# Three more row blocks transposed by DMA at the start of a spectral-gate and gated-MLP kernel

## The chip, the cores and the metric

The kernel runs on one core of a Trainium2 chip. The metric is the device time of one execution in microseconds (us). The kernel before takes 493.05 us, the median of three runs (492.82 to 494.5). Its profiled execution spans 490.9 us.

TensorE (PE) multiplies matrices and writes to PSUM. VectorE (DVE), ScalarE (ACT) and GpSimd (POOL) do elementwise work. SyncE (SP) issues most of the DMA transfers. A row block is 128 of the 2048 rows of the input; there are 16, numbered 0 to 15.

## The reference

x is 2048 x 576. Its rows are normalised; the result goes through a spectral filter (branch A) and through a gated MLP with a spatial mixing matrix (branch B).

```python
def _A_ref(x, w_r, w_i):
    X = rfft2(x)                      # 2048 x 289 complex
    X = X * (w_r + 1j * w_i)
    return irfft2(X).astype(bfloat16)

def _B_ref(x, w_in, w_sp, b_sp, w_out):
    z = _gelu(einsum('bsd,df->bsf', x, w_in))      # 2048 x 4608
    z1 = z[..., :Fh]                               # Fh = 2304
    z2 = _layernorm(z[..., Fh:], axis=-1)
    g = einsum('ts,bsf->btf', w_sp, z2) + b_sp[None, :, None]
    return einsum('bsf,fd->bsd', z1 * g, w_out)

xn = _layernorm(x, axis=-1)
s = _A_ref(xn, A_w_r, A_w_i)
g = _silu(_B_ref(xn, B_w_in, B_w_sp, B_b_sp, B_w_out))
return x + s * g
```

## The kernel before

The first phase normalises each row block, transposes it (the contraction over 576 columns needs the columns on partitions), and feeds it to two users on TensorE: the row transform of branch A (`p0`) and the product with the second half of w_in (`fill`, chunks of z2). The later phases do the column transforms of branch A between further chunks of branch B, then the product with w_sp (`main`), then the product with w_out (`outm`).

One large SBUF tile, AR, is cut into regions by hand. Three buffers hold normalised rows:

```python
XN = [reg("XN", i * KS * P, KS * P) for i in range(3)]
```

The loads at the start: rows 0 to 3, the first two chunks of w_in, then in three thirds the rest of w_in, each followed by a block of four row blocks of x:

```python
for g in range(3):
    third = (WIN2[:, :, 2 * g * ZC:2 * (g + 1) * ZC], slice(Fh + 2 * g * ZC, Fh + 2 * (g + 1) * ZC))
    if g:
        load_win(*third)            # two large and four small transfers on SyncE
    else:
        load_win_tail(*third, nc.gpsimd)
        load_row(3)
        nc.sync.dma_start(out=CDSD, ...)
    load_x(g + 1)                   # row blocks 4g+4 to 4g+7
```

Statistics and reciprocal root of a row block (DVE, and for row blocks from 4 on POOL), its normalisation, and the two ways to transpose it:

```python
def ln1_apply(m):
    xn = XN[m % 3]
    ...                             # two tensor_scalar on DVE: (x - mean) * rs

def xpose_dma(m):
    nc.sync.dma_start_transpose(out=xnT[:, m, :, :], in_=XN[m % 3].rearrange("p (k i) -> p k i", k=KS))

def xpose(m, eng=nc.scalar):
    xn = XN[m % 3]
    pt = psh.tile([P, KS, P], BF16, tag="h")
    for ks in range(KS):            # KS = 5
        nc.tensor.transpose(pt[:, ks, :], xn[:, ks * P:(ks + 1) * P], ident[:])
    ...                             # one eviction to xnT by ACT or DVE
```

The fold makes the sums and differences that the row transform multiplies, and `p0` multiplies them:

```python
def p0_fold(m):                     # two tensor_tensor on DVE
    xe, xo = xnT[:, m, 0:KS - 1:2, :], xnT[:, m, 1:KS - 1:2, :]
    nc.vector.tensor_tensor(out=FS[m % 4][:, 0, :, :], in0=xe, in1=xo, op=ALU.add)
    nc.vector.tensor_tensor(out=FS[m % 4][:, 1, :, :], in0=xe, in1=xo, op=ALU.subtract)

def p0(m, start):                   # four matmuls from FS[m % 4]
    ...
```

The loop over row blocks. DT is the first row block that a DMA transposes (7). The order within each of SyncE, PE and DVE is the order in which the program is written:

```python
for m in range(MT):
    if m % 2 == 0 and 0 < m < DT - 3:
        xpose(m + 3)
    spend(...)
    if m > 1:
        p0_fold(m)
    if m + 5 < MT:
        ln1_stats(m + 5, (0, 1) if m != 1 else (0,))
        if m != 1:
            ln1_aggr(m + 5)
    if m + 4 < MT:
        ln1_apply(m + 4)
        if m == 1:
            ln1_stats(m + 5, (1,))
            ln1_aggr(m + 5)
        if m + 4 >= DT:
            xpose_dma(m + 4)
        ...
    if m % 2 == 0:
        fill(1, 0)                  # four matmuls of a z2 chunk
        if m == 0:
            xpose(3)
        # p0(m), then the 64-row tails of four chunks, then the tails of p0 of m and m + 1
        fill(1, 0, lambda: p0_pair(m), lambda: p0(m, True) if m else None)
    else:
        p0(m, False)
        p0_out(m)                   # ACT evicts, POOL (or SyncE from 11 on) writes Ad
        fill(1, 0)
        if m + 3 < DT:
            xpose(m + 3)
        fill(1, 0)
```

The output stage. `outm` leaves the multiplication with y, the addition of x and the store of the last row block of an output group to a list `later`, and `main` of the next unit (one unit is seven products of eight matmuls each) works it off:

```python
prod(b, "P6", tb[u, 0])
add(p1a, b, p1)
...
prod(c, "P5", zblk(p, 0, 1))
prod(b, "P7", tb[u, 1], True)       # waits for the add above, which reads b
add(p1, b, p1b)
u_sum(1, 1, c, p1)
while later:
    later.pop()()
prod(a, "P2", zblk(p, 1, 0), True)
...
prod(c, "P3", zblk(p, 1, 1), True)
u_sum(1, 0, c, ux)
u_gate(1, 0)
tsum(u + 1, 1)
```

Of the kernel before, what the change touches and what calls it, by code (L numbers as in the profile page):

```python
# [14 lines left out]
P = 128  # L15
# [75 lines left out]
def kernel(  # L91
# [12 lines left out]
    nc = tc.nc  # L104
# [5 lines left out]
    KS = (D + P - 1) // P  # L110
# [57 lines left out]
    def reg(name, off, n):  # L168
        return AR[:, offs[name] + off: offs[name] + off + n]
# [12 lines left out]
    CESO = reg("CESO", P, 8 * QD).rearrange("p (c r d) -> p c r d", c=2, r=4)  # L182
    BF = take_(offs["G4"] + N2 * P - 8 * P, 8 * QD).bitcast(F32).rearrange("p (v a d) -> p v a d", v=2, a=2)
    MM = reg("MM", 0, 3 * P).rearrange("p (a k) -> p a k", a=3)
    XN = [reg("XN", i * KS * P, KS * P) for i in range(3)]
    YST = [reg("STG", i * D, D) for i in range(3)]
    PST = [reg("BES", i * 4 * LE, 4 * LE) for i in range(8)]
    AIN = [reg("AIN", i * 8 * L, 8 * L) for i in range(4)]
# [35 lines left out]
    def load_x(c):  # L224
        nc.sync.dma_start(out=XC[c], in_=xv[:, 4 * c:4 * c + 4, :])
# [32 lines left out]
    load_win_main(*wh[0], nc.sync, (1,))  # L258
    load_row(2)
    load_win_main(*wh[1], nc.sync, (1,))  # L260
    for g in range(3):
        third = (WIN2[:, :, 2 * g * ZC:2 * (g + 1) * ZC], slice(Fh + 2 * g * ZC, Fh + 2 * (g + 1) * ZC))
        if g:
            load_win(*third)
        else:
            load_win_tail(*third, nc.gpsimd)
            load_row(3)
            nc.sync.dma_start(out=CDSD, in_=cd_cdsd.ap().rearrange("p (a k l) -> p a k l", a=2, k=3))
        load_x(g + 1)
    def rstd_of(mv, n, tag, eng=nc.gpsimd):  # L270
        ve = small.tile([P, n], F32, tag=tag + "v")
        eng.tensor_scalar(out=ve[:], in0=mv[:, :, 1], scalar1=1e-5, scalar2=one[:, 0:1], op0=ALU.add, op1=ALU.mult)
        rs = small.tile([P, n], F32, tag=tag + "r", bufs=5)
        nc.gpsimd.tensor_tensor(out=rs[:], in0=ve[:], in1=mhalf[:, 0:n], op=ALU.pow)
        return rs
# [18 lines left out]
        ln1_stats(m)  # L294
        ln1_aggr(m)

    DT = 7
    st1 = {}
    ln1_of = {}

    def ln1_apply(m):
        xn = XN[m % 3]
        mean, rs = ln1_of[m]
        xr = XC[m // 4][:, m % 4, :].rearrange("p (a d) -> p a d", a=2)
        nc.vector.tensor_scalar(out=xn[:, 0:4 * P].rearrange("p (b a i) -> p a b i", b=2, a=2),
                                in0=xr[:, :, 0:2 * P].rearrange("p a (b i) -> p a b i", b=2), scalar1=mean, scalar2=rs,
                                op0=ALU.subtract, op1=ALU.mult)
        nc.vector.tensor_scalar(out=xn[:, 4 * P:KS * P].rearrange("p (r a i) -> p r a i", r=2, a=2),
                                in0=xr[:, None, :, 2 * P:H2].to_broadcast((P, 2, 2, HT)), scalar1=mean, scalar2=rs,
                                op0=ALU.subtract, op1=ALU.mult)  # L310

    def xpose_dma(m):
        nc.sync.dma_start_transpose(out=xnT[:, m, :, :], in_=XN[m % 3].rearrange("p (k i) -> p k i", k=KS))

    def xpose(m, eng=nc.scalar):
        xn = XN[m % 3]
        pt = psh.tile([P, KS, P], BF16, tag="h")
        for ks in range(KS):
            nc.tensor.transpose(pt[:, ks, :], xn[:, ks * P:(ks + 1) * P], ident[:])  # L319
        if eng is nc.scalar:  # L320
            nc.scalar.activation(out=xnT[:, m, :, :], in_=pt[:], func=ACT.Identity)
        else:
            eng.tensor_copy(out=xnT[:, m, :, :], in_=pt[:])  # L323
# [301 lines left out]
    def main(u):  # L625
        it, p = units[u]
        t0, nt = ITS[it]
        a, b, c = (psh.tile([P, 512], F32, tag="h", name="pm")[:, 0:nt] for i in range(3))
        B = [BB[:, h * (S // 2) + t0:h * (S // 2) + t0 + nt] for h in range(2)]
        p1, p1a, p1b, ux = (PT[4 * (u % 2) + i][:, 0:nt] for i in range(4))  # L630
        zb = Z1B[u % 2]

        def prod(dst, name, z, more=False):
            for s in range(HM):
                nc.tensor.matmul(dst, lhsT=z[:, s, :], rhs=SLB[SA[name]][:, s, 0:nt], start=(s == 0 and not more),  # L635
                                 stop=(s == HM - 1), skip_group_check=more)

        def add(out, x, y):
            nc.vector.tensor_tensor(out=out, in0=x, in1=y, op=ALU.add)  # L639

        def u_sum(f, h, x, y):
            add(U[:, 2 * p + f, h, 0:nt], x, y)

        def u_gate(f, h):
            o = U[:, 2 * p + f, h, 0:nt]
            nc.vector.tensor_tensor(out=o, in0=o, in1=zb[:, f, h, 0:nt], op=ALU.mult)  # L646

        prod(a, "P1", zblk(p, 0, 0))
        nc.scalar.activation(out=p1, in_=a, func=ACT.Identity)  # L649
        nc.gpsimd.tensor_tensor(out=p1b, in0=p1, in1=B[1], op=ALU.add)  # L650
        prod(b, "P6", tb[u, 0])
        add(p1a, b, p1)
        nc.gpsimd.tensor_tensor(out=ux, in0=p1a, in1=B[0], op=ALU.add)  # L653
        while later and not u:
            later.pop()()
        tsum(u + 1, 0)
        prod(c, "P5", zblk(p, 0, 1))
        prod(b, "P7", tb[u, 1], True)
        add(p1, b, p1b)
        u_sum(1, 1, c, p1)  # L660
        while later:
            later.pop()()
        prod(a, "P2", zblk(p, 1, 0), True)
        tsum(u + 1, 2)
        u_sum(0, 0, a, B[0])
        prod(b, "P4", tb[u, 2], True)
        u_sum(0, 1, b, p1b)
        u_gate(1, 1)
        u_gate(0, 0)
        u_gate(0, 1)  # L670
        prod(c, "P3", zblk(p, 1, 1), True)
        u_sum(1, 0, c, ux)
        u_gate(1, 0)
        tsum(u + 1, 1)

    def load_xy(m, b):
        nc.sync.dma_start(out=YIN[b], in_=Yd[m * P:(m + 1) * P, :])
# [2 lines left out]
    later = []  # L680
# [72 lines left out]
    with tc.manual_schedule(engines={SP, PE, DVE}):  # L753
# [48 lines left out]
        for m in range(MT):  # L802
            if m % 2 == 0 and 0 < m < DT - 3:
                xpose(m + 3)
            spend(0.9 if m + 3 < DT else 0.6, 0.5 + 0.6 * (m + 4 < MT) + 1.0 * (m + 5 < MT))
            if m > 1:
                p0_fold(m)
            if m + 5 < MT:
                ln1_stats(m + 5, (0, 1) if m != 1 else (0,))
                if m != 1:  # L810
                    ln1_aggr(m + 5)
            if m + 4 < MT:
                ln1_apply(m + 4)
                if m == 1:
                    ln1_stats(m + 5, (1,))
                    ln1_aggr(m + 5)
                if m + 4 >= DT:
                    xpose_dma(m + 4)
                if m + 5 == MT:
                    nc.sync.dma_start(out=G1, in_=cd_g1.ap().rearrange("p (s k) -> p s k", s=N2))  # L820
            if m % 2 == 0:
# [6 lines that stand above are left out]
                p0_out(m)  # L828
# [4 lines that stand above are left out]
# [123 lines left out]
```

## Time and profile before

| | |
|---|---|
| time, median of 3 | 493.05 us |
| span of the profiled execution | 490.9 us |
| PE busy | 483.8 us |
| DVE busy | 332.0 us |
| POOL busy | 204.6 us |
| ACT busy | 159.9 us |
| mean DMA rate | 147 GB/s |
| granted TensorE clock | 0.999 |

Reading: the profile is of one execution. A group in it is named by its line of the kernel, its engine and operation, and out<-in by the program's tile names, with the shape of one instruction and how many there are. In a list in order of time the columns are the start in us from the start of the span, the duration in us, then the group; in square brackets stands how long its engine had been idle before it and what ended that. A list of waits gives the total in us, the number of waits and the longest. PE is TensorE's matmuls, PEld its weight loads, SPq SyncE's queue of DMA issues. L329 and L330 are the fold, L305 and L308 the normalisation, L281 and L285 the statistics, L319 a transpose on PE, L321 its eviction on ACT, L347 the product of the row transform, L339 its 64-row tail, L476 the z2 chunks, L313 the DMA transposes, L354 the writes of Ad; L635 and L639 are the products and adds of `main`, L696 and L697 the deferred finish.

The two stretches that the change touches are the first 45 us and the starts of the second and third output group, near 305 and 413 us.

### The profile page before, as it was taken

Reading aid. Unit: us, or ns where it says so; the run is one execution under the profiler, and the core shown is the slowest. Engines: PE = TensorE matmul, PEld = TensorE weight load, DVE = VectorE, ACT = ScalarE, POOL = GpSimd, SP = SyncE. Lnnn points to the kernel's source line nnn. Section 1 sums busy time; section 2 is a strip of 40 time slices with the busy share of each in tenths; the row PEclk is TensorE's granted clock in tenths of the full one; section 3 lists DMA queues with packets and bytes.
Section 4 is the critical chain, followed back from the end, with each engine's and each line's share of the span. In section 5 each row is a group of like instructions: output and inputs, shape, how many; then the busy total and the mean of one; then the engine's idle time right before and its main releaser. Section 6 shows DMA issues by size and latency. Waiting matters only on the chain.

```text
span 490.9 us, 9286 instructions
## 1 busy us (share of the span) xinstructions
PE 483.8 (99%) x3407; PEld 305.9 (62%) x3407; DVE 332.0 (68%) x739; ACT 159.9 (33%) x335; POOL 204.6 (42%) x272
## 2 busy tenths in 40 slices
PE   8999999999999999999999999999999999999996
PEld 3555454555555444566665677566666678888885
DVE  7996388798876989866666527666566416877632
ACT  4767877867767565100000111000000011000001
POOL 3581134434523784454454311553553312666600
PEclk9999999999999999999999999999999999999999
DMA  8878889988464999841111996111211872111212
GB/s 279 232 142 213 254 296 278 330 237 236 133 248 121 273 257 254 278 148 33 54 44 34 184 184 161 45 34 39 59 33 43 167 174 71 52 45 46 72 38 60
DMA packets 94461, 72.13 MB, mean 147 GB/s; under 512 B 45904, under 2 KB 86608, under 8 KB 94160
## 3 DMA queue, kind: packets, MB, share of 16 engines
q1 hardware_dynamic: 88832, 57.95, 44.7%
q0 software_dynamic: 4896, 13.17, 8.2%
q8 instruction: 26, 0.43, 0.4%
q10 hardware_dynamic: 688, 0.43, 0.3%
q14 instruction: 19, 0.16, 0.1%
HBM read 40.40 MB, written 21.26 MB: 126 GB/s over the span
## 4 chain that ended last, share of the span: by engine, by line
PE 96%; DVE 2%; DMA 1%; issue 0%; SPq 0%; ACT 0%; DVEq 0%
PE pm L635 44%; PE ph L476 15%; PE ph L572 14%; PE po L691 13%; PE pa L347 2%; PE pb L404 2%; PE pa L420 1%; PE pa L446 1%; PE pa L368 1%; PE pl L691 1%; PE pa L392 1%; DMA AR<-in_A_x_dram 1%; PE pa L439 0%; DVE AR L696 0%; PE pt L319 0%; DVE AR L639 0%
## 5 line engine op out<-in xcount | busy, mean ns | idle before, releaser
L635 PE MATMUL pm<-AR,Z_74 128*128 128x384 bf16 (+1 forms) x864 | 138.8, 309 | 0.0
L639 DVE TENSOR_TENSOR AR<-pm,AR 128x384 f32<-128x384 f32 (+3 forms) x162 | 82.3, 513 | 73.7 <-PE pm L635 70.5
L635 PEld LDWEIGHTS <-Z_74 128*128 128x128 bf16 x864 | 84.5, 98 | 40.6
L635 PE MATMUL pm<-AR 128*128 128x384 bf16 (+1 forms) x648 | 107.1, 309 | 0.6 <-DVE AR L639 0.6
L476 PE MATMUL ph<-AR 128*128 128x384 bf16 (+1 forms) x480 | 87.3, 327 | 0.6 <-DVE AR L323 0.5
L572 PE MATMUL ph<-AR 128*128 128x512 bf16 (+1 forms) x360 | 84.8, 379 | 0.0
L635 PEld LDWEIGHTS <-AR 128*128 128x128 bf16 x648 | 63.3, 98 | 31.3 <-DVE AR L621 0.6
L649 ACT ACTIVATE AR<-pm 128x384 f32<-128x384 f32 (+1 forms) x27 | 12.3, 455 | 185.9 <-PE pm L635 185.9
L691 PE MATMUL po<-AR 128*128 128x288 bf16 x540 | 66.6, 286 | 0.0
L691 PEld LDWEIGHTS <-AR 128*128 128x128 bf16 x594 | 56.9, 98 | 14.0
L476 PEld LDWEIGHTS <-AR 128*128 128x128 bf16 (+1 forms) x480 | 39.6, 97 | 38.6 <-issue 16.7
L623 POOL TENSOR_TENSOR AR<-Z_74,AR 128x1024 bf16<-128x1024 bf16 x26 | 55.3, 2126 | 13.6 <-PE pm L635 12.2
L592 POOL DMA_DIRECT2D Z1d<-AR x55 | 32.0, 582 | 57.5 <-ACT AR L581 56.1
L650 POOL TENSOR_TENSOR AR<-AR 128x384 f32<-128x384 f32 (+1 forms) x27 | 22.9, 848 | 78.5 <-ACT AR L649 76.0
L581 ACT ACTIVATE AR<-ph 128x512 bf16<-128x512 f32 x72 | 41.8, 595 | 19.8 <-PE ph L572 19.6
L572 PEld LDWEIGHTS <-AR 128*128 128x128 bf16 (+1 forms) x360 | 30.3, 97 | 27.6 <-issue 4.1
L495 ACT ACTIVATE Z_74<-ph 128x384 bf16<-128x384 f32 x72 | 33.7, 498 | 20.8 <-PE ph L476 20.4
L696 DVE TENSOR_TENSOR AR<-AR 128x576 bf16<-128x576 bf16 (+2 forms) x18 | 9.7, 541 | 39.9 <-ACT AR L694 39.9
L653 POOL TENSOR_TENSOR AR<-AR 128x384 f32<-128x384 f32 (+1 forms) x27 | 30.7, 1136 | 12.9 <-DVE AR L639 12.9
L694 ACT ACTIVATE AR<-po 128x576 bf16<-128x576 f32 x15 | 9.8, 650 | 76.7 <-PE po L691 76.7
L646 DVE TENSOR_TENSOR AR<-AR 128x384 bf16<-128x384 bf16 (+1 forms) x108 | 31.3, 332 | 0.9
L699 POOL DMA_DIRECT2D out_dram<-AR x12 | 6.6, 548 | 49.9 <-DVE AR L697 42.1
(188 smaller groups left out, 472.1 us busy)
## 6 DMA issues: line engine op xcount, KB each, us to landing
Z1d<-AR POOLq DMA_DIRECT2D x55, 128.0 KB, 3.9
AR<-Z1d SPq DMA_DIRECT2D x36, 192.0 KB, 3.0
AR<-in_A_x_dram SPq DMA_DIRECT2D x20, 144.0 KB, 3.1
AR<-in_B_w_in_dram SPq DMA_DIRECT2D x14, 192.0 KB, 3.9
AR<-in_B_w_out_dram SPq DMA_DIRECT2D x1, 2592.0 KB, 11.4
AR<-Ad SPq DMA_DIRECT2D x4, 578.0 KB, 6.8
AR<-in_A_w_r_dram SPq DMA_DIRECT2D x16, 144.5 KB, 3.9
AR<-in_A_w_i_dram SPq DMA_DIRECT2D x16, 144.5 KB, 3.8
```

The lines of the kernel that those rows point to most:

```text
L476: nc.tensor.matmul(self.ph[:], lhsT=xnT[rows, self.m, ks, :], rhs=WIN2[rows, ks, n * ZC:(n + 1) * ZC], start=start, stop=stop)
L495: nc.scalar.activation(out=zc, in_=ph[:], func=ACT.Gelu_apprx_tanh)
L572: nc.tensor.matmul(self.ph[:].rearrange("p (a t) -> p a t", a=4), lhsT=wb[rows, ks, (fi % WG) * P:(fi % WG + 1) * P], rhs=xnT[rows, 4 * tq ...
L581: nc.scalar.activation(out=zs, in_=ph[:], func=ACT.Gelu_apprx_tanh)
L592: (nc.sync if place[0] > len(kinds) - 16 else nc.gpsimd).dma_start(out=d, in_=s_)
L623: (nc.gpsimd if u else nc.vector).tensor_tensor(out=t, in0=zblk(p, 1, 0), in1=t2, op=ALU.subtract)
L635: nc.tensor.matmul(dst, lhsT=z[:, s, :], rhs=SLB[SA[name]][:, s, 0:nt], start=(s == 0 and not more), stop=(s == HM - 1), skip_group_check= ...
L639: nc.vector.tensor_tensor(out=out, in0=x, in1=y, op=ALU.add)
L646: nc.vector.tensor_tensor(out=o, in0=o, in1=zb[:, f, h, 0:nt], op=ALU.mult)
L650: nc.gpsimd.tensor_tensor(out=p1b, in0=p1, in1=B[1], op=ALU.add)
L653: nc.gpsimd.tensor_tensor(out=ux, in0=p1a, in1=B[0], op=ALU.add)
L691: nc.tensor.matmul(pv[:, hh, :], lhsT=U[:, fi, h, i * P:(i + 1) * P], rhs=WOUT[:, fi, c0 + hh * H2:c0 + hh * H2 + w // nh], start=(fi == 0 ...
```

## The change

Row blocks 4, 5 and 6 are transposed by DMA instead of by PE and ACT: DT goes from 7 to 4. Normalised rows get six buffers instead of three (the three new ones lie in a region that is free until the z1 chunks). The last third of w_in, and the block of x after it, are loaded behind the transpose of row block 5 instead of ahead of all transposes. The folds of row blocks 2 and 3 move to between the statistics of a later row block and the next normalisation. In the output stage the deferred finish moves to the end of the unit. The aim is to take transposes and evictions off TensorE and ScalarE, to let the DMA transposes start before the last third of w_in fills the DMA queue, and to keep folds and the deferred finish from standing in front of what TensorE waits for.

```diff
-    XN = [reg("XN", i * KS * P, KS * P) for i in range(3)]
+    XN = [reg(n_, i * KS * P, KS * P) for n_ in ("XN", "ZT") for i in range(3)]
@@ loads
-    for g in range(3):
+    def load_third(g):
         third = (WIN2[:, :, 2 * g * ZC:2 * (g + 1) * ZC], slice(Fh + 2 * g * ZC, Fh + 2 * (g + 1) * ZC))
         ...
         load_x(g + 1)
+
+    for g in range(2):
+        load_third(g)
@@ row blocks
-    DT = 7
+    DT = 4
-        xn = XN[m % 3]
+        xn = XN[m % 6]
@@ main
         u_sum(1, 1, c, p1)
-        while later:
-            later.pop()()
         prod(a, "P2", zblk(p, 1, 0), True)
         ...
         tsum(u + 1, 1)
+        while later:
+            later.pop()()
@@ the loop over row blocks
-            if m > 1:
+            if m >= DT:
                 p0_fold(m)
             if m + 5 < MT:
                 ln1_stats(m + 5, (0, 1) if m != 1 else (0,))
                 if m != 1:
                     ln1_aggr(m + 5)
+            if 1 < m + 1 < DT:
+                p0_fold(m + 1)
             if m + 4 < MT:
                 ln1_apply(m + 4)
                 ...
                 if m + 4 >= DT:
                     xpose_dma(m + 4)
+                if m == 1:
+                    load_third(2)
```

(cut: the same change of `m % 3` to `m % 6` in both transposes)

## The prediction

> **What bounds the kernel now.** I read the page first: busy time by engine and the chain that ended last.
>
> ```profile
> span 490.9 us, 9286 instructions
> PE 483.8 (99%) x3407; PEld 305.9 (62%) x3407; DVE 332.0 (68%) x739; ACT 159.9 (33%) x335; POOL 204.6 (42%) x272
> ...
> PE 96%; DVE 2%; DMA 1%; issue 0%; SPq 0%; ACT 0%; DVEq 0%
> ```
>
> TensorE (PE) is the path: 483.8 of 490.9 us. Time can come only from work taken off PE or from its stalls, so next I asked who made PE wait, over the whole span:
>
> ```profile
> PE pw L757 <- DVE Z_74 L220: 1.2, 1, 1.2
> PE pm L635 <- DVE AR L639: 0.6, 1, 0.6
> PE ph L476 <- DVE AR L323: 0.5, 1, 0.5
> PE pa L347 <- DVE AR L329: 0.5, 1, 0.5
> PE pt L319 <- DVE AR L305: 0.3, 1, 0.3
> ```
>
> The change touches two of these waits: the 0.5 us for a fold (line 329) and the 0.6 us of the last output stage (line 639). The start (pw, first pt, first ph) stays as it is. Then PE in order of time around the fold wait:
>
> ```profile
> 18.27 0.50 PE L476 MATMUL ph<-AR 64*128 64x384 bf16 x4
> 18.61 0.41 PE L339 MATMUL pa<-AR 64*128 64x290 bf16 x4
> 19.53 0.67 PE L347 MATMUL pa<-AR 128*128 128x290 bf16 x4 [0.51 <-DVE AR L329]
> 20.04 0.81 PE L476 MATMUL ph<-AR 128*128 128x384 bf16 x4
> 20.68 0.44 PE L319 MATMUL pt<-ident,AR 128*128 128x128 bf16 x5
> 20.96 2.11 PE L476 MATMUL ph<-AR 128*128 128x384 bf16 x12
> ...
> 23.50 0.50 PE L476 MATMUL ph<-AR 64*128 64x384 bf16 x4
> ```
>
> Line 319 is the transpose of one row block. Its record lasts 0.44 us, but the next matmul starts 0.28 us after it: in the stream it costs 0.28, because tails of matmuls overlap. The tails groups (the 64-row x4 groups) beat the time, one per two row blocks: they start at 13.05, 18.27, 23.50, 27.88, 32.25. Without transposes the beat is 4.37; the two before are 5.22 and 5.23.
>
> How full the other resources are there:
>
> ```profile
> 10.00:15.00 5.00, 5.00 (x42) 2.67 (x39) 4.34 (x16) 3.01 (x7) 1.64 (x5) 1.00 1.08 322
> 15.00:20.00 5.00, 4.45 (x39) 2.65 (x39) 4.45 (x18) 3.95 (x9) 3.70 (x7) 1.00 1.10 323
> 20.00:25.00 5.00, 5.00 (x41) 3.05 (x40) 4.61 (x18) 3.50 (x8) 2.85 (x6) 1.00 0.45 115
> ```
>
> Columns: PE, weight load, DVE, ACT, POOL busy, granted clock, DMA share, GB/s. DVE is about 90% busy throughout; the DMA engines are full until 20 us, then half empty.
>
> [...]
>
> **The change on PE.** Three transposes leave (rows 4, 5, 6): 3 x 0.29 = 0.87 us. Row 4's also waited for its normalised row: the four matmuls before it start at 14.29, need 4 x 0.163 = 0.65, and the transpose starts at 15.14, so 0.2 us of stall leaves. The fold wait is worth 19.53 - 18.27 = 1.26 against the undisturbed 28.56 - 27.88 = 0.68: 0.58. Check: 0.58 + 0.2 of transposes and stall in the first long beat (excess 0.85), 0.28 + 0.58 in the second (excess 0.86). At most 0.87 + 0.2 + 0.58 = 1.65 us early. Three ACT evictions of 0.76 us also go; ACT is not on the path.
>
> **The change on DVE.** It loses no work, only order. From the start-to-start times one row block costs statistics 0.85, aggregate 0.13, normalise 0.55, fold 0.41: 1.94 us, against 4.37 / 2 = 2.19 us on PE. What held the fold of row 3 before:
>
> ```profile
> 18.64 0.41 DVE L305 TENSOR_SCALAR AR<-AR,mv_292,rs 128x512 bf16<-128x512 bf16 x1 [0.48 <-PE ph L476]
> ...
> 19.19 0.29 DVE L329 TENSOR_TENSOR AR<-AR 128x256 bf16<-128x256 bf16 x1
> ```
>
> Normalising row 6 started when POOL's rs for it ended (18.03 + 0.57 = 18.60; the named PE is a near coincidence), and the fold stood behind it. Now the fold goes first. Adding up from 15.22: half the statistics of row 6 to 15.6, fold 2 to 16.0, normalise 5 to 16.6 (data written to 16.75), rest of the statistics and aggregate to 17.1, statistics and aggregate of 7 to 18.1, fold 3 first half done 18.4. PE, 0.78 us earlier, is ready for it at 17.49 + 0.68 = 18.17. So 0.3 us of the 0.58 stays; row 3's product starts at 18.47 instead of 19.53: 1.06 us gained there. Then fold 4 at 20.6, fold 5 at 22.5, both just in time for PE (row 4 at 21.57, row 5 at 22.84); fold 6 is wanted at 24.5.
>
> **The new queue on SyncE.** Before, the transposes had an emptied queue:
>
> ```profile
> L313 SPq DMA_TRANSPOSE AR<-AR x9: 1199/1226/1792, 21.6 to 37.4; - x9
> ...
> DMA to landing us min/median/max: 2.6/4.1/6.2
> ```
>
> Now the order is transpose 4, transpose 5, two big and four small loads of the last third of w_in, the last block of x, transpose 6. Transpose 4 issues when row 4 is normalised, 15.33, and lands near 18; transpose 5 issues at 16.8 and lands near 19.5 to 20. The loads issue from 18.05, six at 0.46 us each (13.82 to 15.59 before), x at 20.8, transpose 6 at 21.25. As data: the last third took from 16.05 (landing of the x block ahead) to 19.60, 3.5 us, and x from 19.60 to 22.12, 2.5 us, beside two Ad writes. Starting near 19.4, the third is in by 22.5 to 23, x by 24.5 to 25, transpose 6 (640 packets of 256 bytes at 21 ns in the packet records: 0.85 us of 16 engines) with Ad writes beside it near 26. The third is wanted by PE only at 24.8 (row 0's fifth chunk, 26.15 before): fits.
>
> Transpose 6 does not fit. Fold 6 waits from 24.5 to 26.0, row 6's product starts at 26.35 instead of its free 26.0, and fold 7 comes one DVE row later: 26.05 + 1.94 + 0.29 = 28.3, where PE would be at 27.6. Row 7's product then starts at 28.3, against 28.56 before. After that DVE gains 0.25 us a row and PE runs free. So of 1.06 us about 0.25 is left, 0 to 1.0 for transpose 6 landing between 26.3 and 25.0.
>
> **The last output stage.** The deferred finish (lines 696, 697) moves from the middle of the next unit to its end. Before, it stood from 417.97 to 420.1, blocked by line 623 on POOL until 419.28, and the chain ran over DVE to the 0.64 us stall at 423.03. After: last gate and sum done near 421.05, finish (0.4 each) to 421.9, the add that PE waits for done at 422.35; PE wants it at 422.36. If line 650 on POOL (421.15 to 421.89) holds the finish, it ends 0.5 later. Gain 0.1 to 0.6, say 0.35. The same move at 311.6 meets units of 9.1 us with slack: nothing.
>
> **Sum.** 0.25 + 0.35 = 0.6, plus some weight on a transpose 6 that lands earlier than I add up: 0.95. 493.05 - 0.95 = 492.1.
>
> **Rivals.** First, everything goes through: no DVE wait, both stalls vanish: 1.65 + 0.6, 490.8 us. For it: DVE still leads PE by 2 us at fold 6 (25.26 against 27.29). Against: 1.5 us of queue added ahead of transpose 6. Second, the queue hits harder: Ad writes of 4 to 7 us to landing squeeze transpose 6 past 27, DVE passes the delay to every later row until it has caught up, and PE loses 1 us on balance: 494. Third, the last third of w_in comes after 24.8, and PE waits there directly: 0 to 1 us lost, while DVE catches up meanwhile: 492.5 to 493.5. Fourth, the early gain is undone later by a DMA-paced step (the reads of Ad before the first column stage): the first read lands at 56.66, its matmul starts at 57.95, so 1.3 us of slack speaks against.
>
> **Range and chances.** All of it moves within 2 us of 493, far below 2% (9.9 us). Nothing in the rest of the program changes: the order on PE differs only by the 15 matmuls. 80% range 490.8 to 493.3; faster by over 2% 0.01, same 0.98, slower 0.01.
>
> **What would show it.** Right: DVE's fold line waits 1 to 2 us for a DMA on AR near 25 us; PE's line for the row products waits for the fold at rows 6 and 7, 0.3 to 0.7 us each; the tails beat from 13 to 18.3 shrinks to 4.5; the last-stage wait for line 639 falls below 0.5. Wrong: no DMA wait on the folds (first rival), a PE wait for w_in (third), or tails groups after 32 us that are later than before (second).

## The result and the profile after

The changed kernel takes 497.11 us (median of 4 runs, 496.82 to 498.08) against 492.94 us for the kernel before on the same chip: a ratio of 1.0081, 95% interval 1.0056 to 1.0107. It is slower, by about 4 us. The predicted 492.1 us and its range, 490.8 to 493.3, both miss.

The page of the kernel after first. In part 2, PEclk is the granted TensorE clock in tenths for 40 slices of the span.

```profile
span 495.0 us, 9261 instructions
...
PE 484.7 (98%) x3392; PEld 305.8 (62%) x3392; DVE 331.2 (67%) x739; ACT 158.6 (32%) x332; POOL 204.7 (41%) x272
...
PEclk9989999999999999999999999999999999999999
...
PE 89%; DMA 6%; DVE 4%; issue 1%; POOL 0%; ACT 0%; DVEq 0%; POOLq 0%
```

TensorE has 15 matmuls fewer and yet 0.9 us more busy time; its clock is below full in the third slice (24.8 to 37.1 us), and DMA has 6% of the chain that ended last, where it had 1%. Who made PE wait (columns: us in total, times, longest):

```profile
PE pa L351 <- DVE AR L333: 3.1, 2, 2.6
...
PE pm L639 <- DVE AR L643: 0.4, 1, 0.4
```

After the load section a line of the kernel after is 4 higher than before: L351 is the row product (was L347), L333 the fold (L329), L317 the DMA transpose (L313), L343 the tails (L339), L480 the z2 chunks (L476). The fold wait, 0.5 us before, is 3.1 us now. The chain in order of time (start, us, what) says what the fold waited for:

```profile
15.50 5.72 DMA AR<-AR
...
22.36 6.57 DMA AR<-AR
...
29.37 1.15 PE pa L351 x4
```

These two DMAs are the transposes of row 4 (15.50 to 21.22) and of row 6 (22.36 to 28.93). VectorE stands still for the second one; this is the fold of row 6:

```profile
29.02 0.29 DVE L333 TENSOR_TENSOR AR<-AR 128x256 bf16<-128x256 bf16 x1 [3.86 <-DMA AR<-AR]
```

TensorE in order of time:

```profile
18.53 0.67 PE L351 MATMUL pa<-AR 128*128 128x290 bf16 x4
...
21.67 0.67 PE L351 MATMUL pa<-AR 128*128 128x290 bf16 x4
...
23.54 0.67 PE L351 MATMUL pa<-AR 128*128 128x290 bf16 x4 [0.53 <-DVE AR L333]
24.05 2.76 PE L480 MATMUL ph<-AR 128*128 128x384 bf16 x16
29.37 1.15 PE L351 MATMUL pa<-AR 128*128 128x290 bf16 x4 [2.56 <-DVE AR L333]
30.45 0.82 PE L480 MATMUL ph<-AR 64*128 64x384 bf16 x4
31.06 0.69 PE L343 MATMUL pa<-AR 64*128 64x290 bf16 x4
31.69 0.95 PE L351 MATMUL pa<-AR 128*128 128x290 bf16 x4
...
35.07 0.66 PE L351 MATMUL pa<-AR 128*128 128x290 bf16 x4
```

The L351 lines are the products of rows 3, 4, 5, 6, 7 and 8. The products of rows 6, 7 and 8 in the kernel before:

```profile
27.29 0.66 PE L347 MATMUL pa<-AR 128*128 128x290 bf16 x4
...
28.56 0.67 PE L347 MATMUL pa<-AR 128*128 128x290 bf16 x4
...
31.66 0.66 PE L347 MATMUL pa<-AR 128*128 128x290 bf16 x4
```

At row 6 the same four matmuls last 1.15 us instead of 0.66, at row 7 0.95, at row 8 0.66 again. The windows say why (columns as in the prediction; behind the five pairs of busy time stands the granted clock, 1.00 in the first line):

```profile
28.00:28.50 0.50, 0.00 (x0) 0.00 (x0) 0.00 (x0) 0.00 (x0) 0.00 (x0) 1.00 2.25 380
28.50:29.00 0.50, 0.00 (x0) 0.00 (x0) 0.00 (x0) 0.00 (x0) 0.00 (x0) 0.88 0.10 26
29.00:30.00 1.00, 0.63 (x3) 0.43 (x4) 0.97 (x4) 0.00 (x0) 0.00 (x0) 0.50 1.28 304
...
31.00:32.00 1.00, 1.00 (x8) 0.38 (x5) 1.00 (x4) 1.00 (x3) 0.81 (x1) 0.50 0.59 107
32.00:32.50 0.50, 0.50 (x5) 0.34 (x4) 0.47 (x3) 0.50 (x1) 0.03 (x1) 0.71 0.57 114
```

The starts of the row products, before and after:

| row | before | after | difference |
|---|---|---|---|
| 3 | 19.53 | 18.53 | -1.00 |
| 5 | 24.18 | 23.54 | -0.64 |
| 6 | 27.29 | 29.37 | +2.08 |
| 7 | 28.56 | 31.69 | +3.13 |
| 8 | 31.66 | 35.07 | +3.41 |
| last matmul of the program ends | 487.16 | 490.67 | +3.51 |
| span | 490.9 | 495.0 | +4.1 |

So the early gain is there. Then 2.7 us go at row 6 (2.56 of them the wait), 1.3 at the halved clock between rows 6 and 8. Behind that some 0.4 us go in the column stages (waits for the multiplies of line 398), 0.27 come back in the output stage, and the closing part after the last matmul is 0.6 us longer.

### The profile page after: what moved, and what is told of

Its sections match the earlier page's. It is cut to its first block, busy times and chain, and to the rows that moved or that the text cites. A ratio compares the mean times of both kernels' runs of the same rounds, so it can differ in the third digit from the quotient of the medians.

```text
span 495.0 us, 9261 instructions
## 1 busy us (share of the span) xinstructions
PE 484.7 (98%) x3392; PEld 305.8 (62%) x3392; DVE 331.2 (67%) x739; ACT 158.6 (32%) x332; POOL 204.7 (41%) x272
## 4 chain that ended last, share of the span: by engine, by line
PE 89%; DMA 6%; DVE 4%; issue 1%; POOL 0%; ACT 0%; DVEq 0%; POOLq 0%
PE pm L639 44%; PE po L695 13%; PE ph L576 13%; PE ph L480 12%; DMA AR<-AR 2%; DMA AR<-in_B_w_in_dram 2%; PE pa L351 1%; PE pa L424 1%; PE pb L408 1%; PE pa L450 1%; PE pa L372 1%; PE pl L695 1%; DMA AR<-in_A_w_i_dram 1%; PE pa L396 1%; DMA AR<-in_A_x_dram 1%
## 5 line engine op out<-in xcount | busy, mean ns | idle before, releaser
L480 PE MATMUL ph<-AR 128*128 128x384 bf16 (+1 forms) x480 | 87.5, 328 | 0.8 <-DVE AR L327 0.5
L480 PEld LDWEIGHTS <-AR 128*128 128x128 bf16 (+1 forms) x480 | 39.8, 97 | 39.7 <-issue 17.9
L585 ACT ACTIVATE AR<-ph 128x512 bf16<-128x512 f32 x72 | 41.9, 596 | 19.7 <-PE ph L576 19.5
L700 DVE TENSOR_TENSOR AR<-AR 128x576 bf16<-128x576 bf16 (+2 forms) x18 | 7.6, 424 | 39.9 <-ACT AR L698 39.9
L398 DVE TENSOR_TENSOR AR<-pa,AR 128x578 bf16<-128x578 f32 x32 | 22.8, 752 | 6.7 <-PE pa L396 3.9
## 6 DMA issues: line engine op xcount, KB each, us to landing
AR<-in_A_w_r_dram SPq DMA_DIRECT2D x16, 144.5 KB, 3.6
AR<-in_A_w_i_dram SPq DMA_DIRECT2D x16, 144.5 KB, 3.7
```

Source lines behind the costliest of these rows:

```text
L480: nc.tensor.matmul(self.ph[:], lhsT=xnT[rows, self.m, ks, :], rhs=WIN2[rows, ks, n * ZC:(n + 1) * ZC], start=start, stop=stop)
L585: nc.scalar.activation(out=zs, in_=ph[:], func=ACT.Gelu_apprx_tanh)
```

## The experiments

The theory in its first form: the DMA transposes land later than predicted because they share the queue and the engines with loads and with GpSimd's writes of the row products to `Ad`, and the wait that follows halves TensorE's clock. Rivals: the clock is the larger part; the last third of w_in is; the rest of the change is. Ratios are against the kernel before on the same chip (medians 493.28 to 493.49 us), with 95% intervals.

### The clock, the third of w_in, and the rest of the change

**e1_warm**: dummy matmuls ahead of row 6's product, nothing else.

```diff
-                fill(1, 0, lambda: p0_pair(m), lambda: p0(m, True) if m else None)
+                fill(1, 0, lambda: p0_pair(m), lambda: (keep_warm(10) if m == 6 else None, p0(m, True) if m else None))
```

> The changed kernel with ten 512-column matmuls on a zero tile put in front of row 6's product, where PE waits 2.56 us. They take about 2.2 us of that wait, so PE is idle at most 0.5 us at a time. Theory (the wait costs twice: 2.56 us of idle and about 1.3 us of the halved clock that follows): no slice under full clock near 30 us, the step from row 6's product to row 7's falls from 2.32 to about 1.3 us, and the time falls by 1.0 to 1.4 us to about 495.9 us. Rival (the clock record is of no account, the wait alone costs): 497.1 us or a little more.

Measured: 497.04 us, 1.0069 (1.0050 to 1.0088). The clock stays at full rate (1.00 in every window of 1 us from 12 to 40 us). Row 6's transpose lands 0.2 us later (29.13) and its product starts at 29.57; from there to row 8 (34.55) it takes 4.98 us, where the kernel after took 5.70 and the kernel before 4.37. So 0.7 of the 1.3 us belonged to the clock alone. The other 0.6 stay: with full clock, row 7's product waits for its own transpose, which lands at 30.97. Later, 0.59 us are lost in a wait for VectorE at 103.3 us. The gain of 1.0 to 1.4 us that was expected is not to be seen in the time: 497.1 us was the rival's figure. With these intervals a gain of half a microsecond could not be told.

**e2_third_first**: the last third of w_in and the x block loaded ahead of all transposes again.

```diff
-    for g in range(2):
+    for g in range(3):
         load_third(g)
@@
-                if m == 1:
-                    load_third(2)
```

> The changed kernel with the last third of w_in and the last block of x loaded ahead of all transposes, as before the change; rows 4 to 6 still by DMA. Theory (what counts is what stands ahead of a transpose in SyncE's queue): now transpose 4 is the one behind the loads: it lands near 23 to 24 instead of 21.2, fold 4 waits 3 us instead of 0.6, row 4's product waits 2 us, but transposes 5 and 6 follow it closely (25 and 26) and fold 6 waits little. Time 494 to 497 us. Rival (DMA transposes are slow in this stretch whatever stands ahead): the same waits as in the changed kernel at row 6, 497 us.

Measured: 496.88 us, 1.0077 (1.0052 to 1.0101): the loss only moves. Row 4's transpose, issued at 16.68, lands at 25.45, and TensorE waits there (the profiled execution, at 499.35 us, is the slowest of five, so these landings are late ones):

```profile
25.90 0.67 PE L351 MATMUL pa<-AR 128*128 128x290 bf16 x4 [3.06 <-DVE AR L333]
```

**e3_third_later**: the third behind the transpose of row 6 (`if m == 2` in place of `if m == 1`).

> The changed kernel with the last third of w_in one row block later, behind transpose 6. Theory of the queue: transpose 6 issues near 20 and lands by 23.5 to 24, fold 6 no longer waits; the third lands 2 us later than now, at 26 to 28, so PE waits 1 to 2 us for w_in, and transpose 7 now stands behind it, so fold 7 waits 2 to 4 us. Time 494.5 to 497.5 us, with the wait of 2.5 us at row 6 gone. Rival (transposes slow by themselves): fold 6 still waits 3 us or more and the time is over 497.5 us.

Measured: 495.43 us, 1.0043 (1.0027 to 1.0059). Row 6's transpose, with neither load ahead of it, takes 19.18 to 21.82, 2.6 us, and row 6 does not wait; but the transpose of row 4, with neither the third nor the last x block near it, still takes 15.43 to 20.83. So what delays the first transposes is not the third. TensorE now waits 0.93 us for w_in at 26.2 and 0.92 us for row 7's transpose at 29.5.

**e4_rest_alone**: the DMA transposes and the load order of before (DT = 7, third first), with the six buffers, the early folds and the moved finish.

> The rest of the change alone: rows 4 to 6 transposed by PE and the last third loaded first, as before; six buffers, the moved folds of rows 2 and 3 and the moved finish stay. Theory (all of the loss is from the three DMA transposes): no DMA wait of a fold before 35 us, the 0.5 us wait of row 3's product smaller, the wait in the last output stage 0.4 us; 0.3 to 0.9 us faster than before, 492.0 to 492.7 us. Rival (the new order costs something itself): 493.5 us or more.

Measured: 492.89 us, 0.9992 (0.9985 to 0.9998). The rest of the change is worth some 0.4 us. The whole loss comes with the three transposes.

### Ad writes beside the transposes

In the traces so far the transposes land in company: 21.22 beside an `Ad` write that lands at 21.40; in e3 20.83 and 21.36 beside one at 21.08. The packet records of the kernel after add to this: of the 640 packets of 256 bytes of row 4's transpose 548 start before 18.0, and the last has passed at 18.49, but the sixteen increments of its semaphore all come between 20.61 and 21.22. So its data had passed more than 2 us before it counted as landed, and the last increment comes 0.18 us ahead of the landing of GpSimd's write at 21.40. That the one waits for the other is the author's guess from these times. Theory A, then: the `Ad` writes hold the transposes' completion back. Rival Q: it is SyncE's own queue.

**e6_ad_late** and **e7_ad_late_third_later** were meant to issue the writes of rows 0 to 5 later:

```diff
-        (nc.gpsimd if m < 11 else nc.sync).dma_start(out=Adw[m], in_=sg[:, :, 0:L])
+        held_out.append((m, sg))
+        while m >= 6 and held_out:
+            q, s_ = held_out.pop(0)
+            (nc.gpsimd if q < 11 else nc.sync).dma_start(out=Adw[q], in_=s_[:, :, 0:L])
```

> The kernel after with one thing moved: the writes of the row products of rows 0 to 5 to Ad in DRAM are issued only once row 6's product is out, so none is in flight while the transposes of rows 4 and 5 are; nothing is left out. Theory A (the transposes' completion is held back by the Ad writes beside them): the transpose of row 4, issued near 15.5 us, lands by 18.7 instead of 21.2, row 5's by 20.0 instead of 21.6, the last third of w_in and the x block 1.5 to 2.5 us earlier, the transpose of row 6 at 26.0 to 27.0 instead of 28.9; the row product of row 6 waits under 0.7 us instead of 2.56, the clock does not halve, and the time is 493.0 to 494.6 us. Rival Q (it is the queue that the transposes stand in: the x block ahead of them, the third behind them): row 4's transpose still lands after 20.5, row 6's product still waits 2 us or more, the time is 496.3 to 497.5.

> As the run before, and the last third of w_in issued behind the transpose of row 6 as well (which alone took 495.4 us, with waits of 0.93 us for w_in at 26.2 and 0.92 us for the transpose of row 7 at 29.5). Theory A: the transposes of rows 4, 5, 6 land by 18.7, 20.0 and 22.0; the third, whose own 4.7 us are no shorter, still comes 0.5 to 0.9 us late, and row 7's transpose 0 to 0.5 late: 494.3 to 495.2 us. Rival Q: rows 4 and 5 land after 20.5 as with the third moved alone, and the time stays at 495.2 to 495.8.

They test nothing: the kernel sets only the order of SP, PE and DVE by hand, and GpSimd's first two writes still go out at 15.55 and 16.34 (e7: 15.92 and 16.71), where the kernel after has 15.64 and 16.43. 497.99 us (1.0086, 1.0070 to 1.0101) and 497.51 us (1.0078, 1.0061 to 1.0096) are readings of the kernel after and of e3 once more; that e7 is 2 us above e3 shows how far such a queue varies from build to build. Their transposes again land beside the second write: 21.32 and 21.48, 21.70 and 21.70.

**e8_ad_held** adds to the edit of e6, with the third where the kernel after has it, one copy on VectorE for which the writes truly wait:

```diff
         held_out.append((m, sg))
+        if m == 6:
+            col = AR[:, offs["BES"]:offs["BES"] + 24 * LE].rearrange("p (i c) -> p i c", c=4 * LE)[:, :, 0:1]
+            nc.vector.tensor_copy(out=col, in_=col)
         while m >= 6 and held_out:
```

> The run meant to hold the Ad writes of rows 0 to 5 back had not done so: the writes were issued at 15.6 and 16.3 us as in after, since GpSimd's instructions are placed as soon as their inputs are there. Here they truly wait: one VectorE copy of a column of the six staging buffers onto itself, placed after the sixth row's fold, must come first. Nothing is left out. Theory A (the transposes' completion is held back by Ad writes in flight): the transpose of row 4, issued near 15.5, lands by 19.0 instead of 21.2, row 5's by 20.3, the transpose of row 6 by 27.3 instead of 28.9, the row product of row 6 waits under 1 us instead of 2.56; 493.0 to 495.0 us, unless the six writes issued together near 28 us hold back the transposes of rows 9 to 11 (another 0 to 1.5 us). Rival Q (the queue in which the transposes stand, with the x block ahead and the third behind): row 4's transpose still lands after 20.5, row 6's product still waits 2 us or more, 496.5 us or more.

Measured: 499.35 us, 1.0129 (1.0112 to 1.0146), slower still, for two reasons. First, the transposes of rows 4 and 5 do land early, as A has it (15.31 to 18.55, 17.57 to 20.20), and the third's last piece at 24.56 instead of 26.20; but the x block still comes at 27.30, the transpose of row 6 at 28.03, and row 6 waits 2.49 us. For that wait Q is right. Second, the six held writes in one burst block GpSimd. Its timeline:

```profile
30.93 4.41 POOL L366 DMA_DIRECT2D Ad<-AR  x6
35.38 0.50 POOL L276 TENSOR_SCALAR ve<-mv,one 128x1 f32<-128x1 f32 x2
```

and VectorE's, where the next normalisation stands 3 us for the scale factor that GpSimd owes it:

```profile
36.44 0.41 DVE L309 TENSOR_SCALAR AR<-AR,mv,rs 128x512 bf16<-128x512 bf16 x1 [3.02 <-POOL rs L278]
```

**b5d_ad_held** and **b4d_ad_held** put the same hold into the forms with the third first (rows 5 and 6, and rows 4 to 6, by DMA).

> The form with rows 5 and 6 transposed by DMA and the third loaded first (492.34 us, waits of 0.29 and 0.10 us for row 5's transpose at 23.5) with the Ad writes of rows 0 to 5 held back in the same way. Theory A: row 5's transpose lands by 22.2 instead of 23.4, its wait is gone, 491.9 to 492.4 us. Rival Q: it lands at 23.4 as before, 492.2 to 492.7. If the held writes then collide with later transposes: a wait near 33 us and 492.8 or more.

> All three rows by DMA with the third loaded first (496.88 us, row 4's transpose 16.68 to 25.45, a wait of 3.06 us), with the Ad writes of rows 0 to 5 held back. Theory A: row 4's transpose lands by 22.3, a wait of 0 to 0.7 us instead of 3.06; 492.2 to 493.8 us. Rival Q: still behind the third and the x block, landing after 24.5, wait of 2 us or more, 495.5 to 497.5.

Measured: 493.96 us (1.0015, 1.0005 to 1.0026) and 497.24 us (1.0079, 1.0054 to 1.0103). The landings follow A: row 5's transpose in the first at 22.30 instead of 23.42, row 4's in the second at 22.18 instead of 25.45, and TensorE waits 0.64 us at row 4 instead of 3.06 (0.53 at row 5 in both). The second comparison sets the fastest of six executions beside the slowest of five, so its size is uncertain. Neither form is faster for it, and the burst shows again: waits of 1.55 us at 33.6 in the first, of 1.92 us at 35.2 in the second.

**e5_third_act_queue**: the last third from ScalarE's queue.

```diff
-                    load_third(2)
+                    load_third(2, nc.scalar)
```

> After with the last third of w_in alone issued from ScalarE's queue instead of SyncE's. Rival Q: with no third between them in its queue, the x block lands by 25.5 and the transpose of row 6 by 27.0, row 6's product waits under 0.8 us, 494.0 to 495.3 us. Theory A (and with it a common limit of the 16 engines): the transposes of rows 4 and 5 land near 21.2 and 21.6 as before whatever the queue, and the third shares the engines with the x block, so the transpose of row 6 lands at 27.5 to 29 and the time is 496.0 to 497.5 us. In either case the issue on ScalarE, 0.4 to 0.8 us each for six transfers, delays the activations near 18 to 22 us.

Measured: 498.61 us, 1.0106 (1.0083 to 1.0129), and not the test that was meant. ScalarE's place is not set by hand either: its issues moved up, the last to 13.0 us, held ScalarE, and TensorE waited for an eviction. The first of its waits (columns as above):

```profile
PE pt L324 <- ACT Z L500: 3.0, 1, 3.0
```

### Fewer transposes

**b6_one_more** and **b5_two_more**: row 6, and rows 5 and 6, by DMA, the third first, the rest of the change kept.

```diff
-    DT = 4
+    DT = 6        # and 5
+    FD = 4        # the folds of rows 2 and 3 stay early
```

> A milder form: only row 6 is transposed by DMA (before: from row 7 on), the last third of w_in and the x block loaded first as in before, folds of rows 2 and 3 moved ahead, six buffers, the moved finish of the output stage. Theory A and rival Q alike: the transpose of row 6 is issued near 19 to 20 behind an x block that lands near 20.8, comes in by 22.5 to 25.0, and its fold is not needed before 25.5, so no wait; the TensorE loses five transposes, 0.29 us, against the kernel with all the rest and no DMA transpose added (492.89 us): 492.3 to 492.9 us. If the longer closing part (0.62 us) comes with any added DMA transpose, it is 492.9 to 493.4.

> As the run before with row 5 transposed by DMA as well. Its transpose is issued near 17 behind the third of w_in and beside two Ad writes. Both theories let it come late: Q because the third (landing near 19.5) and the x block (20.8) stand ahead of it in the queue, so 22.5 to 24; A because the Ad writes land near 22 to 23 beside it. Row 5's fold is needed near 23.7: a wait of 0 to 0.8 us. Time 492.2 to 493.3 us; with a wait above 1.5 us, 493.8 or more, the transposes cost as much as in the kernel after.

Measured: 492.94 us, 0.9989 (0.9979 to 1.0000), and 492.34 us, 0.9981 (0.9970 to 0.9991). Both are slightly faster than the kernel before, but not clearly faster than e4 (0.9985 to 0.9998), which has no transpose more. The third one, row 4's, is what the kernel has no room for at the place where it stands.

### Both causes, one at a time and together

Two edits that hold back the same transfers without a burst. The x block of rows 12 to 15 goes behind the transpose of row 7:

```diff
-        load_x(g + 1)
+        if g < 2:
+            load_x(g + 1)
@@
                 if m + 4 >= DT:
                     xpose_dma(m + 4)
+                if m == 3:
+                    load_x(3)
```

and the `Ad` writes of rows 0 to 2 go out from SyncE, behind the transposes of rows 8 to 10 (`held_out` is an empty dictionary at the start):

```diff
+        if m < 3:
+            held_out[m] = sg
+        else:
+            (nc.gpsimd if m < 11 else nc.sync).dma_start(out=Adw[m], in_=sg[:, :, 0:L])
@@
+                if m - 4 in held_out:
+                    nc.sync.dma_start(out=Adw[m - 4], in_=held_out[m - 4][:, :, 0:L])
```

With the load order of the kernel after: **e9_x_behind** (x), **e11_ad_sync** (Ad), **e10_x_behind_ad_sync** (both).

> After with only the x block of rows 12 to 15 moved: issued behind the transpose of row 7 instead of ahead of the transpose of row 6. If the x block ahead of it is what holds the transpose of row 6: it lands 0.6 us after the third's last piece, near 26.8 instead of 28.9, row 6's product waits 0.3 to 0.9 us instead of 2.56, the clock keeps its full rate, 494.3 to 495.6 us. If it is the Ad write beside it (issued 21.2, landing 26.4 in after) or a common limit of the engines: the transpose lands after 28.2 all the same, a wait of 2 us or more, 496.5 us or more.

> After with only the Ad writes of rows 0 to 2 issued by SyncE behind the transposes of rows 8 to 10. If the two causes act one after the other: row 4's transpose lands by 18.7, row 5's by 20.3, the third by 25.0, the x block still ahead at 26.5 to 27.5 and row 6's transpose at 27.2 to 28.2; its product waits 1.5 to 2.5 us; 495.3 to 497.2 us. If the Ad writes alone were the cause, row 6 waits under 0.7 us: 493.3 to 494.8 us.

> As the run before, and the Ad writes of rows 0 to 2 issued by SyncE behind the transposes of rows 8 to 10 instead of by GpSimd, so no Ad write lies beside the transposes of rows 4 to 6 and GpSimd is not loaded by a burst. If the two causes are the whole of it: row 4's transpose lands by 18.7, row 5's by 20.3, the third by 24.6, row 6's transpose by 25.3, row 6's product waits under 0.2 us; 492.2 to 493.6 us, of which 0.6 is the longer closing part. If row 6 still waits over 1 us a third cause is there: 494.5 us or more.

With the third first: **b4x_x_behind** (x), **b4xa_x_behind_ad_sync** (both), and the x block moved with rows 5 and 6 only, **b5x_x_behind**.

> Rows 4 to 6 by DMA with the third loaded first (496.88 us, a wait of 3.06), only the x block of rows 12 to 15 moved behind the transpose of row 7; the Ad writes as in after. If the x block was the larger part: the transposes of rows 4 to 6 land at 21.7 to 22.3, right behind the two Ad writes (21.4, 21.6 in the form with row 4 on TensorE), a wait of 0.2 to 0.8 us at row 4, 492.4 to 493.5 us. If the Ad writes were the larger part: they land after 23 and the wait is 1.5 us or more, 494.3 us or more.

> Rows 4 to 6 by DMA, the third loaded first (496.88 us with a wait of 3.06), the x block behind the transpose of row 7 and the Ad writes of rows 0 to 2 by SyncE behind the transposes of rows 8 to 10. If both causes are the whole: row 4's transpose lands near 20.8 (0.6 after the third), rows 5 and 6 by 22, no wait of TensorE over 0.2 us, 491.6 to 492.6 us, with the longer closing part in it. If a wait over 1 us stays at rows 4 to 6 or at rows 8 to 11 (the Ad writes now in the transposes' own queue): 493.5 us or more.

> Rows 5 and 6 transposed by DMA, the third loaded first (492.34 us), with the x block of rows 12 to 15 behind the transpose of row 7. If the x block ahead is what holds row 5's transpose: it lands near 21.5 instead of 23.4, the waits of 0.29 and 0.10 us are gone, 491.8 to 492.3 us. If the Ad writes alone (landing 22.8 and 23.2) do: it lands at 23 or later, 492.2 to 492.7 us.

Measured:

| form | neither | x behind | Ad by SyncE | both |
|---|---|---|---|---|
| rows 4 to 6, third behind row 5 (after) | 1.0081 | 1.0053 (1.0038 to 1.0069) | 1.0053 (1.0036 to 1.0071) | 1.0042 (1.0027 to 1.0057) |
| rows 4 to 6, third first | 1.0077 | 1.0019 (1.0009 to 1.0029) | not run | 0.9982 (0.9973 to 0.9991) |
| rows 5 and 6, third first | 0.9981 | 0.9975 (0.9965 to 0.9985) | not run | not run |

In us, in the order of the table: 495.87, 496.54, 495.76; 494.43, 492.52; 492.33. In the first row each edit alone gains 1.4 us, and both together are not clear of either alone.

What the `Ad` writes do shows where the DMA issues of a short stretch are listed with their median us to landing. The kernel after, 15.4 to 17.4 us:

```profile
Ad<-AR POOLq DMA_DIRECT2D x2, 144.5 KB, 4.7
AR<-AR SPq DMA_TRANSPOSE x2, 5.0
```

and e10, 15.4 to 17.7 us, the same two transposes with no write beside them:

```profile
AR<-AR SPq DMA_TRANSPOSE x2, 2.9
```

So A stands for the transposes of rows 4 and 5: they land at 18.62 and 20.26 (e11: 18.99 and 20.63) instead of 21.22 and 21.57. The packet records of e10 say how much of this is the data itself: the last of row 4's 640 packets has passed at 17.98, in the kernel after at 18.49. So of the 2.6 us between the landings 0.5 lie in the data, and 2.1 between the last packet and the increments. Sharing of the engines as the data pass is thus, by these records, the smaller part. That the larger one is a wait for the write beside it is inferred from the landings (21.22 and 21.40) and from the runs without that write; how it comes about no run shows.

What the x block does shows in e9, TensorE in order of time, rows 6 and 7:

```profile
27.60 0.67 PE L352 MATMUL pa<-AR 128*128 128x290 bf16 x4 [0.57 <-DVE AR L334]
...
29.48 0.67 PE L352 MATMUL pa<-AR 128*128 128x290 bf16 x4 [0.53 <-DVE AR L334]
```

Row 6's transpose lands at 27.16, 0.7 us behind the third's last piece, instead of 28.93; the wait is 0.57 us instead of 2.56, and the clock holds (1.00 from 12 to 40 us). In e11, with the x block left ahead, that transpose lands at 29.02 although the two before it were early, and row 6 waits 2.96 us, longer than in the kernel after (waits of TensorE, columns as above; the other one is 0.53 us at row 7):

```profile
PE pa L351 <- DVE AR L333: 3.5, 2, 3.0
```

So moving the `Ad` writes does not help row 6 while the x block stands before it.

In e10 row 6 does not wait, as expected, but the time is 2 us above the expected one: the first `Ad` write left on GpSimd (row 3's, 23.34 to 27.85) now lies beside the transpose of row 7 (23.28 to 28.05), and row 7 waits 0.84 us, row 9 0.85 us, and the first column stage 0.51 us for the reads of `Ad`. The hold moved the collision by three rows. With the third first, the x block is the larger part: in b4x row 4's transpose lands at 22.03 and its product waits 0.76 us, with the `Ad` writes unmoved. And there is room for the held writes: in b4xa TensorE runs through,

```profile
21.77 0.66 PE L352 MATMUL pa<-AR 128*128 128x290 bf16 x4
...
23.36 0.67 PE L352 MATMUL pa<-AR 128*128 128x290 bf16 x4 [0.26 <-DVE AR L334]
...
26.46 0.66 PE L352 MATMUL pa<-AR 128*128 128x290 bf16 x4
...
27.73 0.67 PE L352 MATMUL pa<-AR 128*128 128x290 bf16 x4
```

rows 4 to 7 against 22.91, 24.18, 27.29 and 28.56 before. All three rows are transposed by DMA there, and the kernel is faster than before: with the two causes out of the way the three transposes are no loss at all. The form with the lowest ratio, b5x, takes 492.33 us against 493.34 of before, a quarter of a percent, and beats both kernels; its row 5 no longer waits (its transpose lands at 22.05 instead of 23.42), though its time is not clear of b5's and b4xa's.

## Why the prediction was wrong

**Right.** TensorE's early gain: row 3 at 18.53 where 18.47 was predicted, and the tails beat from 13 to 18 us is 4.37 (predicted 4.5). The kind of loss: the fold waits on a DMA near 25 us, and TensorE on the fold at row 6. The last third of w_in makes TensorE wait nowhere in the kernel after. The moved finish: the last-stage wait goes from 0.64 to 0.44 us, within the 0.1 to 0.6. That GpSimd's instructions hold the finish up is the prediction's reading, which no run tests: before, line 696 took 1.63 us beside line 623 and 0.46 us at 409.95 with GpSimd idle; after, the two instructions of the finish took 0.45 and 0.81 us, both beside line 654 on GpSimd (424.92 to 425.84).

**The step that failed** is the new queue on SyncE, the sum that ends in "transpose 6 ... with Ad writes beside it near 26". Transpose 6 landed at 28.93, and row 6's product waited 2.56 us. Two terms of the sum were too small.

The first is "Transpose 4 issues when row 4 is normalised, 15.33, and lands near 18; transpose 5 issues at 16.8 and lands near 19.5 to 20". The issues were right (15.50, 17.32, the second half a microsecond late); the landings were 21.22 and 21.57. The 2.7 us from issue to landing match the first transpose of before (21.59 to 24.27), beside which two `Ad` writes were just ending, at 22.45 and 22.88. The longer figures in the very line it quoted, up to 6.2 us, were transposes issued beside fresh `Ad` writes (29.14 to 35.32, with writes issued at 29.17 and 30.48), and it did not ask what set them apart. It named the `Ad` writes beside x and transpose 6, not beside transposes 4 and 5. Taking them away gives 18.6 and 20.3, close to the predicted landings.

The second is "the third is in by 22.5 to 23, x by 24.5 to 25". Even with both transposes on time (e8) these came at 24.6 and 27.3, and transpose 6 at 28.0. Starting from the landing of transpose 5 the third takes 4.4 us (20.20 to 24.56) where 3.5 were read off the kernel before, and x 2.7 us where 2.0 were left for it. The 3.5 us were measured from the x block ahead, with the third issued 5 us earlier, so that its first half landed 1.05 us behind that block (17.10 after 16.05); issued at 18.82, with only transpose 5 still ahead of it, the first half lands 2.3 us behind that transpose (22.47 after 20.20).

For the wait at row 6 the second term weighs more. With the first put right and x left ahead, transpose 6 still lands at 28.03 (e8) and 29.02 (e11) and row 6 waits 2.49 and 2.96 us; with x behind and the `Ad` writes left, it lands at 27.16 and row 6 waits 0.57 (e9).

**From there on** the working of the prediction carries: fold 6 stands 3.86 us (25.16 to 29.02) where 1.5 us were added up, and row 6 starts at 29.37 where 26.35 was. e9 is nearly the picture that was drawn, waits of 0.57 and 0.53 us at rows 6 and 7, but with transpose 6 landing 1.2 us later (27.16). Its last matmul ends at 488.27, 1.1 us later than before; with transpose 6 on the predicted time it would, as an estimate from these two figures, have been about level.

**Not in the prediction**: the halved clock. Rows 6 to 8 take 1.3 us longer under it, of which e1 gives 0.7 back in that stretch and nothing measurable in the time. And "Nothing in the rest of the program changes" was too strong. The wait of the column stages (0 to 1 us near 100 us) comes and goes among builds. The length of the closing part changes too: 3.71 us before, 4.33 or 4.34 in the kernel after and in seven others with its 12 DMA transposes, 3.87 to 3.98 in e5, e8 and b4d, and 3.63 in e10, e11 and b4xa, which have the same 12 transposes and the `Ad` writes of rows 0 to 2 on SyncE. So it does not come with the transposes, as some of the expectations supposed. The last store is issued 1.26 us after the last matmul both before and after, so the difference arises behind it; what sets it stays open.

**The rivals.** The second, "the queue hits harder", was the right one; its 494 us was too small because it moved transpose 6 by one microsecond and not by three, and its sign came: the tails group behind row 8's product starts at 35.66 where 32.25 was. The range treated the landing of transpose 4 as known; with 6.2 us, the longest in the quoted line, in place of 2.7 it would have reached past 496 (an estimate: 493.3 and the 3.5 us between them). The chance of staying within 2% was right, and 4 us are 0.8%.

**The budget of the experiments** (ratio less one, times 493 us): after +4.0, with the x block behind +2.6, with the `Ad` writes moved instead +2.6, with both +2.1. In the order with the third first: +3.8, +0.9, and -0.9 with both. The rest of the change alone is -0.4. So the two causes are the whole loss where the third is loaded first. In the order of the kernel after a further 2 us stay; e10 shows waits of that size at rows 7 and 9 and at the reads of `Ad`, but no run takes them away. Where the `Ad` writes are moved, 0.7 us of the gain is the shorter closing part. The conclusion for the third first does not hang on it: the last matmul ends at 486.90 in b4xa, at 487.07 in e4 and at 487.16 before.

## What to carry to other kernels

A transpose by DMA took 2.6 us here with nothing else under way (b4d, row 8) and 5.4 to 5.9 us beside two writes of 144.5 KB (e3, e6, after): before moving one to an earlier place, list what else is in flight between its issue and the time its result is needed, writes of other engines' queues too, and take its duration from a transpose that had the same company, not from the fastest one. The x block left ahead of transpose 6 cost it 1.8 us (28.93 in the kernel after, 27.16 in e9): put data that is needed late (here that block, rows 12 to 15) behind the small transfers that gate the next step. And read the time of a moved load anew: the third's first half landed 2.3 us behind its forerunner when only transpose 5 was ahead of it in the queue (e8), and 1.05 us behind when its issue ran ahead (before). The edit that was to delay the DMAs of GpSimd, whose order is not set by hand, delayed nothing here (e6), and the held burst blocked GpSimd (e8): look at the issue times in the trace before reading the result.

## What the runs showed of the hardware that was not expected

**Between 12 and 40 us each wait of TensorE of more than 2 us was followed by a halved matmul clock for 3.4 us, which began within the wait or up to 2.1 us after it.** In the kernel after TensorE is idle from 26.81 to 29.37 and the granted clock falls at about 28.9, within the wait; in e2 TensorE is idle from 22.84 to 25.90 and the clock falls at about 27.5, in e11 idle from 26.51 to 29.47 and it falls at about 31.6, when TensorE has long been busy again. Adding up the windows of 1 us, the lost share divided by one half, it stays low for 3.38 to 3.42 us in all seven kernels in which it fell. These had one wait of 2.1 to 3.1 us (after, e2, e5, e6, e7, e8, e11); waits up to 1.92 us (b4d, b5d, e3, e9, e10, b4x) left it alone. What sets the moment of the fall no run shows.

**The company of a transpose was worth 2.6 us** (row 4's lands at 21.22 in the kernel after, at 18.62 in e10). Five 128x128 blocks landed 2.6 us after their issue when nothing else was under way (b4d, row 8: 24.27 to 26.84), 3.2 us behind an x block (e8, row 4), 5.4 to 5.9 us beside two writes of 144.5 KB from GpSimd (e3, e6, after). Transposes that queued behind one bulk load landed 0.5 to 0.7 us apart once it was in (e8: 28.03, 28.57, 29.13; b4d: 22.18, 22.78, 23.49), so most of the 2.6 us of one did not hold up the next there.

**GpSimd paid 0.72 to 0.79 us for each `Ad` write it issued** (before and after), and six in a row held its other work for 4.4 us (e8).
